# Scaling the first norm's rows on GpSimd in place of ScalarE, with ScalarE left to empty PSUM

## The chip, the cores and the metric

The kernel runs on one core of a Trainium2 chip. The metric is device time in microseconds (us), median of several runs. Runs of one kernel differ by up to some 7 us (the 11 runs of the kernel before in one set lie from 1665.80 to 1673.18 us), so differences of 2 us or less between times are not read as results. The start of a stage is read from one trace of each kernel. Two traces of this same first stage have it at 36.15 and 36.50 us, so differences of up to some 0.5 us between starts are not read either.

Engine names in the profile: PE is TensorE (matmuls), PEld its weight loads, DVE is VectorE, ACT is ScalarE, POOL is GpSimd. In this kernel the results of matmuls land in PSUM; to empty or evict a PSUM tile is to copy it out, here into YT.

## The reference, cut to what matters

Four layers on x of 2048 tokens by 640 columns. The first is a layer norm, a two-dimensional Fourier filter and a residual:

```python
def _layernorm(x, axis=-1, eps=1e-05):
    m = jnp.mean(x, axis=axis, keepdims=True)
    v = jnp.var(x, axis=axis, keepdims=True)
    return (x - m) / jnp.sqrt(v + eps)
...
    x = A_x
    x = x + _A_ref(_layernorm(x, axis=-1), A_w_r, A_w_i)     # this layer
    x = x + _B_ref(_layernorm(x, axis=-1), ...)              # attention with memory
    ...                                                      # both again
```

The change touches only the norm of the first layer and the transform right after it.

## The kernel before

The 2048 tokens lie as 16 "rows" of 128 partitions by 640 columns. In groups of four rows: DVE computes mean and variance, ScalarE computes Ln and Exp for the reciprocal deviation, five small DVE operations refine it, ScalarE scales each row, PE multiplies it with a table (five column chunks), and each of the five PSUM tiles is emptied into YT, three by DVE and two by ScalarE. The next stage (`along_d`) sums over all of YT, so it can't start before the last tile of the last group is emptied.

```python
def _ln_apply(nc, pool, mv, xin, xout, nt, eps_t, on_dve=False):
    rs = pool.tile([128, 4], FP32, name="lnrs", tag="lnrs")      # pool: two of each in turn ("two-deep")
    nb = pool.tile([128, 4], FP32, name="lnnb", tag="lnnb")
    t, r0 = rs[:, :nt], nb[:, :nt]
    nc.scalar.activation(out=r0, in_=mv[:, :nt, 1], func=ACTF.Ln, bias=eps_t[:, 0:1])
    nc.scalar.activation(out=r0, in_=r0, func=ACTF.Exp, scale=-0.5)
    ...                                                          # four small DVE operations -> rs
    nc.vector.scalar_tensor_tensor(out=nb[:, :nt], ...)          # -mean * rs
    for t in range(nt):
        nc.scalar.activation(out=xout[:, t, :], in_=xin[:, t, :], func=ACTF.Identity,
                             scale=rs[:, t:t + 1], bias=nb[:, t:t + 1])
...
        for q in range(4):
            ...                                                  # statistics of four rows on DVE
            _ln_apply(nc, wk, mv, xt, xn[:, 4 * q:4 * q + 4, :], 4, g["eps"])
            for ch in range(5):
                ps = pp.tile([128, 4, 128], FP32, name="ps1", tag="pa")
                for i in range(4):
                    nc.tensor.matmul(ps[:, i, :], lhsT=xn[:, 4 * q + i, ch * 128:(ch + 1) * 128], ...)
                on_act = ... ch >= 3                             # chunks 3 and 4 on ScalarE
                (nc.scalar.copy if on_act else nc.vector.tensor_copy)(out=YT[...], in_=ps[...])
```

## Time and profile before

| | before |
|---|---|
| median of 4 runs beside the change | 1668.90 us |
| profiled span | 1669.1 us |
| first matmul of the next stage (`along_d`) | 36.15 us |
| ScalarE, one row scaled | 0.91 us |
| DVE, one row scaled (elsewhere in this kernel) | 0.446 us |

The profile's page begins with each engine's busy time, share of the span and number of instructions:

```profile
PE 1564.6 (94%) x14240; PEld 1081.5 (65%) x14241; DVE 810.9 (49%) x2308; ACT 837.0 (50%) x2534; POOL 268.5 (16%) x192
```

PE is busy 94% of the program, but not in its first 36 us. The timeline of that stretch: start in us, duration of the merged piece in us, engine, source line, operation, output from input, how many, and in brackets the idle time ahead of it.

```profile
11.90 3.35 ACT L124 ACTIVATE A1xn_S<-A1x_S,lnnb,lnrs 128x640 bf16<-128x640 bf16 x4 [2.28 <-DVE lnnb L122]
...
15.96 1.07 ACT L247 CAST A1YT_S<-ps 128x512 bf16<-128x512 f32 x2 [0.28 <-PE ps L245]
...
19.75 4.16 ACT L124 ACTIVATE A1xn_S<-A1x_S,lnnb,lnrs 128x640 bf16<-128x640 bf16 x5 [1.43 <-DVE lnnb L122]
...
24.76 2.55 ACT L124 ACTIVATE A1xn_S<-A1x_S,lnnb,lnrs 128x640 bf16<-128x640 bf16 x3
...
27.53 0.21 ACT L113 ACTIVATE lnnb<-lnnb 128x4 f32<-128x4 f32 x1
...
30.48 3.35 ACT L124 ACTIVATE A1xn_S<-A1x_S,lnnb,lnrs 128x640 bf16<-128x640 bf16 x4 [1.40 <-DVE lnnb L122]
...
36.15 6.62 PE L290 MATMUL ab<-A1tab_S,A1YT_S 128*128 128x321 bf16 x30 [1.55 <-DVE A1YT_S L247]
```

ScalarE does rows and evictions by turns: group 0's rows at 11.90, two evictions at 15.96, then rows of two groups from 19.75 to 27.3 with group 1's evictions between, and the last group's rows only at 30.48: its Exp came at 27.53, and its five small operations then stood behind three evictions on DVE until 29.49. The last row is scaled at 33.83 and the next stage starts at 36.15 us. That start is the number to follow.

The view of waits over the first 60 us (who waited for whom: total us, times, longest):

```profile
PE ps L245 <- ACT A1xn_S L124: 22.0, 4, 12.9
...
ACT A1xn_S L124 <- DVE lnnb L122: 5.1, 3, 2.3
```

PE idled 22.0 us there until ScalarE had scaled a row, and ScalarE 5.1 us until the small DVE operations were done.

The groups of instructions by form (busy us, mean ns of one, then idle ahead of them):

```profile
L124 ACT ACTIVATE A1xn_S<-A1x_S,lnnb,lnrs 128x640 bf16<-128x640 bf16 x16 | 13.4, 910 | 5.1 <-DVE lnnb L122 5.1
...
L120 DVE TENSOR_SCALAR bB_S<-bB1x_S,lnmv,lnrs 128x640 bf16<-128x640 bf16 x16 | 7.1, 446 | 0.6
```

The same view of GpSimd alone:

```profile
L329 POOL TENSOR_TENSOR A1tmp_S<-A1gt_S 128x642 bf16<-128x642 f32 x5 | 6.6, 1321 | 2.7 <-DVE A1gt_S L326 2.6
...
L824 POOL MEMSET bB_S<- 128x634 f32 x4 | 2.8, 735 | 60.5 <-PE psg L393 31.1 <-DMA xn<-A1tok_S 29.5
```

ScalarE takes 910 ns a row. DVE takes 446 ns for the same row elsewhere in the kernel. For GpSimd there is no line with a `tensor_scalar` on a large tile: only a `tensor_tensor` of 642 columns (1321 ns) and a memset (735 ns).

### The profile page before, as it was taken

What the parts mean: (1) busy time and instruction counts of PE and PEld (TensorE: products, weight loads), DVE (VectorE), ACT (ScalarE), POOL (GpSimd) and SP (SyncE); (2) the same over time, 40 slices, a digit from 0 to 9 for tenths busy, and PEclk for the clock granted to TensorE, in tenths of its full rate; (3) what the DMA queues carried; (4) which work ended last, traced back from release to release, by engine and by line L of the source; (5) the groups of instructions that cost most, each with busy time, mean ns of one, the idle gap of its engine ahead of it and who ended that gap; (6) DMA issues with size and microseconds to landing.
All of it is one profiled execution on the core that took longest, in us unless ns stands there. A gap on an engine that the chain in (4) does not pass through costs nothing. (4 is left out here: it accounts for less than half of the span.)

```text
span 1669.1 us, 36193 instructions
## 1 busy us (share of the span) xinstructions
PE 1564.6 (94%) x14240; PEld 1081.5 (65%) x14241; DVE 810.9 (49%) x2308; ACT 837.0 (50%) x2534; POOL 268.5 (16%) x192
## 2 busy tenths in 40 slices
PE   4887999999999999999987889999999999999998
PEld 2555666666666666677754666676666666666775
DVE  5963354545555554543357724545555554544111
ACT  5364466666666666511123636666666666663000
POOL 0510111121212121100025001121212121111000
PEclk9997999999999999999999999999999999999999
DMA  4463134434343344633301803434343343437241
GB/s 154 158 237 104 51 137 135 151 114 162 112 161 127 137 147 139 227 129 100 91 17 58 283 2 106 148 116 162 112 160 129 135 149 136 136 123 233 66 127 55
DMA packets 167873, 218.05 MB, mean 131 GB/s; under 512 B 7374, under 2 KB 141836, under 8 KB 159756
## 3 DMA queue, kind: packets, MB, share of 16 engines
q1 hardware_dynamic: 167084, 213.34, 38.2%
q8 instruction: 113, 1.85, 0.4%
q0 software_dynamic: 608, 2.30, 0.4%
q14 instruction: 68, 0.56, 0.1%
HBM read 170.52 MB, written 45.09 MB: 129 GB/s over the span
## 5 line engine op out<-in xcount | busy, mean ns | idle before, releaser
L840 PEld LDWEIGHTS <-bB_S 128*128 128x128 bf16 x3180 | 260.3, 97 | 187.1 <-issue 7.8
L984 DVE TENSOR_TENSOR bB_S<-pso,bB_S 128x480 bf16<-128x480 f32 (+1 forms) x320 | 189.5, 593 | 264.7 <-PE pso L975 249.1
L919 ACT ACTIVATE bB_S<-pss 128x269 bf16<-128x269 f32 (+5 forms) x576 | 213.3, 385 | 192.6 <-PE pss L916 177.8
L1134 PE MATMUL psx<-Wo_sb,bB_S 128*128 128x320 bf16 x2048 | 288.2, 299 | 2.9 <-DMA bB_S<-oTx_d 2.9
L1134 PEld LDWEIGHTS <-bB_S 128*128 128x128 bf16 x2048 | 197.2, 98 | 79.5 <-DMA bB_S<-oTx_d 3.6
L899 DVE CAST bB_S<-psk 128x495 bf16<-128x495 f32 (+3 forms) x320 | 191.4, 599 | 115.9 <-PE psk L840 85.6
L920 DVE TENSOR_TENSOR bB_S<-bB_S,maskf 128x269 bf16<-128x269 bf16 (+5 forms) x576 | 163.1, 287 | 152.6 <-ACT bB_S L919 148.8
L944 POOL TENSOR_TENSOR bB_S<-bB_S,bB_S 128x634 f32<-128x634 f32 x64 | 98.2, 1535 | 821.1 <-ACT bB_S L940 821.1
L908 ACT CAST bB_S<-psv 128x512 bf16<-128x512 f32 (+1 forms) x288 | 160.5, 557 | 84.0 <-PE psv L906 83.7
L884 ACT ACTIVATE bB_S<-psq 128x480 bf16<-128x480 f32 x300 | 152.6, 509 | 98.2 <-PE psq L840 98.2
L840 PE MATMUL psk<-B2hT_S,bB_S 128*128 128x495 bf16 (+3 forms) x800 | 165.0, 342 | 3.7 <-DVE bB_S L899 2.5
L840 PE MATMUL psk<-B1hT_S,bB_S 128*128 128x495 bf16 (+3 forms) x800 | 165.0, 342 | 1.8 <-DVE B1hT_S L1219 1.2
L906 PE MATMUL psv<-bB_S,B2hT_S 128*128 128x256 bf16 x1360 | 163.4, 272 | 0.2 <-DVE bB_S L899 0.2
L906 PE MATMUL psv<-bB_S,B1hT_S 128*128 128x256 bf16 x1360 | 163.4, 272 | 0.2 <-DVE bB_S L899 0.2
L916 PEld LDWEIGHTS <-bB_S 128*128 128x128 bf16 x1216 | 103.0, 98 | 90.1 <-issue 6.4
L840 PE MATMUL psq<-B1hT_S,bB_S 128*128 128x495 bf16 (+5 forms) x780 | 157.6, 336 | 0.1
L840 PE MATMUL psq<-B2hT_S,bB_S 128*128 128x495 bf16 (+5 forms) x780 | 157.6, 336 | 0.1
L916 PE MATMUL pss<-bB_S 128*128 128x132 bf16 (+8 forms) x1216 | 148.3, 216 | 3.1
L906 PEld LDWEIGHTS <-B1hT_S 128*128 128x128 bf16 x1360 | 128.6, 98 | 13.7 <-issue 0.3
L906 PEld LDWEIGHTS <-B2hT_S 128*128 128x128 bf16 x1360 | 128.5, 98 | 13.8 <-issue 0.3
L975 PE MATMUL pso<-bB_S,bB_S 128*128 128x132 bf16 (+8 forms) x1216 | 119.6, 216 | 0.0
L975 PEld LDWEIGHTS <-bB_S 128*128 128x128 bf16 x1216 | 91.2, 98 | 15.7 <-DVE oTmf L985 0.5
(223 smaller groups left out, 1565.7 us busy)
## 6 DMA issues: line engine op xcount, KB each, us to landing
bB_S<-Rd SPq DMA_DIRECT2D x62, 1059.5 KB
oTx_d<-bB_S SPq DMA_DIRECT2D x60, 512.0 KB
bB_S<-oTx_d SPq DMA_DIRECT2D x56, 512.0 KB
bB_S<-in_B_Wq_dram SPq DMA_DIRECT2D x32, 320.0 KB
bB_S<-in_B_Wk_dram SPq DMA_DIRECT2D x32, 320.0 KB
bB_S<-in_B_Wv_dram SPq DMA_DIRECT2D x32, 320.0 KB
bB_S<-oTx_d SPq DMA_DIRECT2D x14, 384.0 KB
Wo_sb<-in_B_Wo_dram SPq DMA_DIRECT2D x4, 1280.0 KB
```

The costliest lines, as they stand in the source:

```text
L840: nc.tensor.matmul(ps, lhsT=w[:, ch, hh * 128:(hh + 1) * 128], rhs=src[:, ch, lo:hi], start=(ch == 0), stop=(ch == 4))
L884: nc.scalar.mul(out=qv[:, :, 0:SEG], in_=x_view(ps, o, n)[:, :, 1:SW], mul=scale)
L899: nc.vector.tensor_copy(out=KTs[h % 2][:, lo:hi], in_=ps[:, 0:hi - lo])
L906: nc.tensor.matmul(ps[:, i * 256:(i + 1) * 256], lhsT=hT[:, ch, (t + i) * 128:(t + i + 1) * 128], rhs=w["Wv"][:, ch, :], start=(ch == 0), ...
L908: nc.scalar.copy(out=V[:, t:t + n, :].rearrange("p a b -> p (a b)"), in_=ps[:, 0:n * 256])
L916: nc.tensor.matmul(ps[:, off - o0:off - o0 + hi - lo], lhsT=KT[:, t * 128:(t + 1) * 128], rhs=QT[:, lo:hi], start=True, stop=True)
L919: nc.scalar.activation(out=E[:, 0:n], in_=ps[:, 0:n], func=ACTF.Exp)
L920: nc.vector.tensor_tensor(out=P[:, o0:o0 + n], in0=E[:, 0:n], in1=bs.mask[:, o0:o0 + n], op=ALU.mult)
L944: nc.gpsimd.tensor_tensor(out=accS, in0=accS, in1=sums_sb, op=ALU.add)
L975: nc.tensor.matmul(pso[:, lo - q0:hi - q0], lhsT=V[:, t, (h % 2) * 128:(h % 2 + 1) * 128], rhs=P[:, off:off + hi - lo], start=(i == 0), st ...
L984: nc.vector.tensor_tensor(out=oT.rearrange("p (r s j) -> p r s j", r=16, j=2)[:, :, s0:s0 + ns, :], in0=byclass(po), in1=rx, op=ALU.mult)
L1134: self.tc.nc.tensor.matmul(ps[:, 0:320], lhsT=lhs(h, k // 2), rhs=self.g["Wo_sb"][:, h, c0:c0 + 320], start=(h == 0), stop=(h == H - 1))
```

## The change

The intent: take the row scaling (13.4 us busy) from ScalarE and give 14 of the 16 rows to GpSimd, which has little to do there; give GpSimd the small operations of four groups too, so that DVE is left mainly with the statistics; let ScalarE alone empty PSUM for the first three groups; and split the last four rows into two pairs, each with one row on DVE and one on GpSimd, so that the last evictions are short. These last pairs' evictions are shared, three by ScalarE and two by DVE.

```diff
--- before.py
+++ after.py
@@ -105,23 +105,22 @@
     nc.vector.bn_aggr(out=mv[:, t, :], in_=st[:, t, :, :])
 
 
-def _ln_apply(nc, pool, mv, xin, xout, nt, eps_t, on_dve=False):
+def _ln_apply(nc, pool, mv, xin, xout, nt, eps_t, small, big):
     rs = pool.tile([128, 4], FP32, name="lnrs", tag="lnrs")
     nb = pool.tile([128, 4], FP32, name="lnnb", tag="lnnb")
     t, r0 = rs[:, :nt], nb[:, :nt]
     nc.scalar.activation(out=r0, in_=mv[:, :nt, 1], func=ACTF.Ln, bias=eps_t[:, 0:1])
     nc.scalar.activation(out=r0, in_=r0, func=ACTF.Exp, scale=-0.5)
-    nc.vector.scalar_tensor_tensor(out=t, in0=mv[:, :nt, 1], scalar=LN_EPS, in1=r0, op0=ALU.add, op1=ALU.mult)
-    nc.vector.tensor_tensor(out=t, in0=t, in1=r0, op=ALU.mult)
-    nc.vector.tensor_scalar(out=t, in0=t, scalar1=-0.5, scalar2=1.5, op0=ALU.mult, op1=ALU.add)
-    nc.vector.tensor_tensor(out=t, in0=t, in1=r0, op=ALU.mult)
-    if on_dve:
-        for t in range(nt):
-            nc.vector.tensor_scalar(out=xout[:, t, :], in0=xin[:, t, :], scalar1=mv[:, t, 0:1], scalar2=rs[:, t:t + 1], op0=ALU.subtract, op1=ALU.mult)
-        return
-    nc.vector.scalar_tensor_tensor(out=nb[:, :nt], in0=mv[:, :nt, 0], scalar=-1.0, in1=rs[:, :nt], op0=ALU.mult, op1=ALU.mult)
+    if small is nc.vector:
+        small.scalar_tensor_tensor(out=t, in0=mv[:, :nt, 1], scalar=LN_EPS, in1=r0, op0=ALU.add, op1=ALU.mult)
+    else:
+        small.tensor_scalar_add(out=t, in0=mv[:, :nt, 1], scalar1=LN_EPS)
+        small.tensor_tensor(out=t, in0=t, in1=r0, op=ALU.mult)
+    small.tensor_tensor(out=t, in0=t, in1=r0, op=ALU.mult)
+    small.tensor_scalar(out=t, in0=t, scalar1=-0.5, scalar2=1.5, op0=ALU.mult, op1=ALU.add)
+    small.tensor_tensor(out=t, in0=t, in1=r0, op=ALU.mult)
     for t in range(nt):
-        nc.scalar.activation(out=xout[:, t, :], in_=xin[:, t, :], func=ACTF.Identity, scale=rs[:, t:t + 1], bias=nb[:, t:t + 1])
+        big[t].tensor_scalar(out=xout[:, t, :], in0=xin[:, t, :], scalar1=mv[:, t, 0:1], scalar2=rs[:, t:t + 1], op0=ALU.subtract, op1=ALU.mult)
 
 
 def _ln_tiles(nc, pool):
@@ -232,20 +231,23 @@
             nc.sync.dma_start(out=self.x, in_=r16(x_src))
         wk = g["ln"]
         pp = tc.alloc_tile_pool(name=f"{self.lname}_ps1", bufs=8, space=PSUM)
-        for q in range(4):
+        groups = [(0, 4), (4, 8), (8, 12), (12, 14), (14, 16)]
+        for q, (a, b) in enumerate(groups):
+            n = b - a
             if xn_src is None:
-                xt = self.x[:, 4 * q:4 * q + 4, :]
+                xt = self.x[:, a:b, :]
                 st, mv = _ln_tiles(nc, wk)
-                for t in range(4):
+                for t in range(n):
                     _ln_stats(nc, st, mv, xt[:, t, :], t)
-                _ln_apply(nc, wk, mv, xt, xn[:, 4 * q:4 * q + 4, :], 4, g["eps"])
+                big = [nc.gpsimd] * 4 if q < 3 else [nc.vector, nc.gpsimd]
+                _ln_apply(nc, wk, mv, xt, xn[:, a:b, :], n, g["eps"], nc.gpsimd if q < 4 else nc.vector, big)
             for ch in range(5):
                 ps = pp.tile([128, 4, 128], FP32, name="ps1", tag="pa")
-                for i in range(4):
-                    nc.tensor.matmul(ps[:, i, :], lhsT=xn[:, 4 * q + i, ch * 128:(ch + 1) * 128], rhs=T[:, 4 * q + i, :], start=True, stop=True)
-                on_act = ch % 2 == 0 if xn_src is not None else ch >= 3
+                for i in range(n):
+                    nc.tensor.matmul(ps[:, i, :], lhsT=xn[:, a + i, ch * 128:(ch + 1) * 128], rhs=T[:, a + i, :], start=True, stop=True)
+                on_act = ch % 2 == 0 if xn_src is not None or q >= 3 else True
                 (nc.scalar.copy if on_act else nc.vector.tensor_copy)(
-                    out=YT[:, ch, :, 4 * q:4 * q + 4, :].rearrange("p g s k -> p s g k"), in_=ps[:].rearrange("p s (g k) -> p s g k", k=8))
+                    out=YT[:, ch, :, a:b, :].rearrange("p g s k -> p s g k"), in_=ps[:, 0:n, :].rearrange("p s (g k) -> p s g k", k=8))
                 if q == 0 and ch == 0:
                     self.tables(gate=YT[0:1, 0, 0, 0, 0:1])
         pp.release()
... (three other call sites: on_dve=True becomes nc.vector, [nc.vector] * n; the operations stay the same)
```

More of the change, by code (lines that the diff above doesn't have):

```diff
@@ L414, in norm @@
             xno = xna[:, 2 * q:2 * q + 2, :]
-            _ln_apply(nc, wk, mv[q], x[:, 2 * q:2 * q + 2, :], xno, 2, g["eps"], on_dve=True)
+            _ln_apply(nc, wk, mv[q], x[:, 2 * q:2 * q + 2, :], xno, 2, g["eps"], nc.vector, [nc.vector] * 2)
             nc.sync.dma_start(out=xnd[:, 2 * q:2 * q + 2, :], in_=xno)
@@ L686, in run @@
                 xno = wk.tile([128, 1, D], BF16, name="xno", tag="xno")
-                _ln_apply(nc, wk, mv, xo, xno, 1, self.g["eps"], on_dve=True)
+                _ln_apply(nc, wk, mv, xo, xno, 1, self.g["eps"], nc.vector, [nc.vector])
                 nc.sync.dma_start(out=self.xnd[:, t, :], in_=xno[:, 0, :])
@@ L1151, in run @@
             _ln_stats(nc, st, mv, x[:, t, :], 0)
-            _ln_apply(nc, self.g["ln"], mv, x[:, t:t + 1, :], xns[t % 3].unsqueeze(1), 1, self.g["eps"], on_dve=True)
+            _ln_apply(nc, self.g["ln"], mv, x[:, t:t + 1, :], xns[t % 3].unsqueeze(1), 1, self.g["eps"], nc.vector, [nc.vector])
         if nxt is not None:
```

## The prediction

> **What bounds it now.** As a whole, TensorE: 1564.6 of 1669.1 us busy, and the chain of waits is 41% PE. The change touches only the first 36 us. There (timeline, waits) PE has 80 small matmuls, 11.5 us, and idles 22.0 us on ScalarE's row scaling. PE's first matmul of the next stage starts at 36.15 us; that is the number to move. It needs all of YT, so everything ahead of it is in series.
>
> By groups of instructions, before 36 us: DVE statistics 32 x 465 ns plus 16 x 195 ns, one row per 0.86 us (5.1 to 22.0 us with evictions between); ScalarE scales 16 rows x 905 ns = 14.5 us, evicts 8 tiles x 587 ns, Ln and Exp 4 x 0.5 us; DVE evicts 12 x 683 ns = 7.5 us. ScalarE serializes scaling and eviction: group 0's rows at 11.9-15.2, then evictions, group 1's not before 19.75, group 2's end at 27.3, group 3's run 30.5-33.8 because its Ln/Exp queued behind and its five small DVE operations took 1.0 us. GpSimd is idle from 18 to 48 us.
>
> **What changes.** 14 of 16 row scalings go to GpSimd, two to DVE (its bf16 row: 445 ns, seen later in the trace). No trace line has a GpSimd tensor_scalar. Its two-input bf16-writing operation on 642 elements took 1321 ns, its memset of 634 fp32 735 ns. The Trainium skill ("GPSIMD Engine Reference", 4.1) puts one-input operations near line rate and two-input ones at a read-port floor; so I estimate 0.8 us a row (0.7 to 1.1). GpSimd small operations: estimate 0.2-0.3 us each with semaphores, 1.0-1.4 us a group, against 1.0 on DVE. ScalarE: minus 14.5 us, plus about 9 more evictions near 0.55. DVE: minus about 6 us of evictions.
>
> **Critical path, estimated.** Group 0: Exp ends 9.6 as before, small operations to 11.0, rows to 14.2 (before 15.2). GpSimd then runs nearly without a break: group 1 with the 1 us indirect DMA to 19.4, group 2 to 23.6, row 13 to 25.4. A new wait: mean/variance tiles are two deep and the rows now read them, so group q+2's aggregates wait for group q's rows. The last pair thus finishes statistics near 25.4, Ln/Exp 26.0, DVE small operations 26.8, row 15 on GpSimd 27.7, half-size evictions to 29.5-30. The next stage starts near 30 in place of 36.15: a gain of about 6 us (range 1 to 9). The later stages aren't changed and should shift one for one: table loads are done by 22 us (DMA is idle from 25 us), and the clock dips (0.5 to 0.6 at 88-96 and 132-152 us) follow PE gaps that shift too.
>
> 6 us of 1669 is 0.35%, near the run-to-run spread (1668.87 to 1673.11). Predicted 1663.5 us, 8 in 10 within 1659.5 to 1668.5. Faster by over 2%: 0.01; within: 0.985; slower: 0.005.
>
> **What would show it.** Next stage's first matmul at 29-31 us. GpSimd rows 0.7-1.1 us each; GpSimd the releaser of the stage's matmuls; DVE statistics of groups 2 on interrupted by waits on GpSimd; ScalarE no longer the wait; span after that point equal to before (1633 us).
>
> **What would make it wrong.** A row on GpSimd at 1.4 us or more makes 14 of them 20 us and eats the gain. Small dependent GpSimd operations at 0.5 us each would cost 2.5 us a group. The shared port: the trace has a DVE two-input operation growing from 0.83 to 2.2 us beside GpSimd work, as the Trainium skill says ("SBUF — State Buffer", port pair as an exclusive lock); the last pairs' DVE row and small operations could stall so. The indirect DMA may sit in GpSimd's queue ahead of rows, waiting for its gate. The stage's end may be set by ScalarE's evictions.

## The result, and the profile after

| | before | after |
|---|---|---|
| median (4 runs each) | 1668.90 us | 1688.47 us |
| ratio | 1 | 1.0112 (1.0094 to 1.0130) |
| profiled span | 1669.1 us | 1686.3 us |
| first matmul of the next stage | 36.15 us | 57.02 us |
| one row on GpSimd | none | 2.49 us from start to start |

A ratio here is the mean time of one kernel's fast runs over that of the other's fast runs of the same rounds, so it isn't quite the ratio of the medians. The change makes the kernel 1.1% slower: 19.6 us by the medians, where about 5 us faster had been predicted.

The same line of the page after:

```profile
PE 1562.4 (93%) x14240; PEld 1080.8 (64%) x14241; DVE 804.2 (48%) x2286; ACT 829.5 (49%) x2533; POOL 309.2 (18%) x226
```

PE's busy time has not grown (1562.4 against 1564.6 us): the loss is idle time. The timeline of the first stage after, columns as before:

```profile
11.78 9.98 POOL L123 TENSOR_SCALAR A1xn_S<-A1x_S,lnmv,lnrs 128x640 bf16<-128x640 bf16 x4
...
14.36 0.61 PE L247 MATMUL ps<-A1xn_S 128*128 128x128 bf16 x4 [14.36 <-POOL A1xn_S L123]
...
22.14 1.07 ACT L249 CAST A1YT_S<-ps 128x512 bf16<-128x512 f32 x2 [9.15 <-PE ps L247]
...
23.32 5.00 POOL L123 TENSOR_SCALAR A1xn_S<-A1x_S,lnmv,lnrs 128x640 bf16<-128x640 bf16 x2
...
29.58 4.99 POOL L123 TENSOR_SCALAR A1xn_S<-A1x_S,lnmv,lnrs 128x640 bf16<-128x640 bf16 x2
...
36.13 9.97 POOL L123 TENSOR_SCALAR A1xn_S<-A1x_S,lnmv,lnrs 128x640 bf16<-128x640 bf16 x4
...
46.48 2.54 ACT L249 CAST A1YT_S<-ps 128x512 bf16<-128x512 f32 x5 [8.80 <-PE ps L247]
48.87 0.25 ACT L113 ACTIVATE lnnb<-lnnb 128x2 f32<-128x2 f32 x1
...
50.41 5.17 POOL L123 TENSOR_SCALAR A1xn_S<-A1x_S,lnmv,lnrs 128x640 bf16<-128x640 bf16 x2
...
57.02 5.65 PE L292 MATMUL ab<-A1tab_S,A1YT_S 128*128 128x321 bf16 x30 [0.46 <-ACT A1YT_S L249]
```

GpSimd's pieces follow one another with small operations, one indirect DMA and one standstill between: four rows in 9.98 us, two in 5.00, two in 4.99, four in 9.97, two in 5.17. Those are the 14 rows, 35.1 us in sum. PE now starts at a row's end (14.36), does 0.6 us of work and idles for the next one. ScalarE, freed for evictions, has its first one at 22.14, six us later than before, as all four rows of group 0 must be there.

A second, smaller thing can be read at the end. Row 13's Exp (48.87) could have run long before: its Ln had begun at 37.34 and took 0.34 us. In ScalarE's queue it stood behind the five evictions of group 2 (46.48), and these waited for the last row of group 2. So GpSimd, which had only begun its small operations for row 13, stood still for 2.85 us until 49.27.

The waits over the first 70 us:

```profile
PE ps L247 <- POOL A1xn_S L123: 41.3, 14, 14.4
ACT A1YT_S L249 <- PE ps L247: 33.2, 5, 9.8
DVE lnmv L105 <- POOL A1xn_S L123: 27.2, 3, 10.9
```

The releaser of PE has changed from ScalarE (22.0 us) to GpSimd (41.3 us). DVE waits 27.2 us for GpSimd: this is the new wait for the two-deep statistics tiles that the prediction named (there are two of each, so a group's statistics wait until GpSimd has read those of the group two before it). It is large in sum, but whether it costs anything is another question, since GpSimd, the engine that is late, was busy nearly all the while (39.0 of the 45 us from 12 to 57).

The groups by form in the first 57 us:

```profile
L123 POOL TENSOR_SCALAR A1xn_S<-A1x_S,lnmv,lnrs 128x640 bf16<-128x640 bf16 x14 | 35.1, 2517 | 0.5
...
L123 DVE TENSOR_SCALAR A1xn_S<-A1x_S,lnmv,lnrs 128x640 bf16<-128x640 bf16 x2 | 0.9, 446 | 0.6 <-POOL lnrs L121 0.6
```

The same instruction on the same data takes 2517 ns on GpSimd and 446 ns on DVE.

The loss comes from the first stage alone. Marks that lie later are shifted by a nearly constant amount: the first matmul of `along_d` from 36.15 to 57.02 (20.9 us), the first of the second layer A from 852.3 to 872.0 (19.7 us).

### The profile page after: what moved, and what is told of

Read it like the earlier page. It is cut to its first block, busy times and chain, and to the rows that moved or that the text cites. A ratio compares the mean times of both kernels' runs of the same rounds, so it can differ in the third digit from the quotient of the medians.

```text
span 1686.3 us, 36214 instructions
## 1 busy us (share of the span) xinstructions
PE 1562.4 (93%) x14240; PEld 1080.8 (64%) x14241; DVE 804.2 (48%) x2286; ACT 829.5 (49%) x2533; POOL 309.2 (18%) x226
```

## The experiments

Theory A: a row costs about 2.49 us on GpSimd by itself, and the number of rows on GpSimd times that sets the first stage. Rival B: the two-deep statistics tiles and the order in ScalarE's queue make the loss. Rival C: GpSimd was slowed by DVE, with which it shares memory ports. A fourth possibility was that the dependent small operations on GpSimd make it. All runs gave a correct result by the comparison with the reference. Each set of runs has its own chip and its own runs of the kernel before; these had medians 1669.16 us (first set), 1667.70 (second) and 1668.95 (third).

### Forms of GpSimd operations, measured by themselves

```diff
+            for i in range(3):
+                G.tensor_scalar(out=pb[i], in0=v, scalar1=e, scalar2=e, op0=ALU.subtract, op1=ALU.mult)
+            ... (three each of the other forms, on one row v of 640 columns, into dead memory)
```

> The kernel before, with GpSimd operations on 128x640 added in the last phase of the program, where DVE and GpSimd are almost idle; results go to dead memory. Theory A (the operation itself is slow on GpSimd, whatever runs beside it): the two-operation form of the change, two pointer scalars, bf16 to bf16, again takes 2.4 to 2.5 us from start to start, and its 320-column form about half, 1.25 to 1.35. Rival C (GpSimd was slowed by sharing memory ports with the busy DVE in the first stage): the same form takes about 1 us here. What in the form costs is open: if it is the second operation, the one-operation form takes 1.3 us or less; if it is the pointer scalars, the form with immediates does; if it is the bf16 data, the fp32 forms do. The plain copy should be near 0.8 us, the tensor_tensor near 1.3 to 1.5. The time of the whole kernel: within 3 us of before.

The kernel took 1669.82 us (one run). The groups by form, GpSimd alone, from 1522 to 1590 us; the letters after the operation are output from input, where `eps` means a scalar read through a pointer (or, in L1134, spread over the row as the second tensor):

```profile
L1118 POOL TENSOR_SCALAR bB_S<-bB2x_S,eps 128x640 bf16<-128x640 bf16 x3 | 7.6, 2537 | 0.1
L1128 POOL TENSOR_SCALAR bB_S<-bB_S,eps 128x640 bf16<-128x640 f32 x3 | 7.5, 2501 | 0.0
L1130 POOL TENSOR_SCALAR bB_S<-bB_S,eps 128x640 f32<-128x640 f32 x3 | 7.5, 2499 | 0.1
L1124 POOL TENSOR_SCALAR bB_S<-bB2x_S 128x640 bf16<-128x640 bf16 x3 | 7.1, 2359 | 0.0
L1122 POOL TENSOR_SCALAR bB_S<-bB2x_S,eps 128x640 bf16<-128x640 bf16 x3 | 5.6, 1888 | 0.0
L1126 POOL TENSOR_SCALAR bB_S<-bB2x_S 128x640 bf16<-128x640 bf16 x3 | 5.4, 1814 | 0.0
...
L1120 POOL TENSOR_SCALAR bB_S<-bB2x_S,eps 128x320 bf16<-128x320 bf16 x3 | 4.3, 1433 | 0.0
L1132 POOL TENSOR_TENSOR bB_S<-bB2x_S 128x640 bf16<-128x640 bf16 x3 | 3.8, 1254 | 0.0
L1134 POOL TENSOR_TENSOR bB_S<-bB2x_S,eps 128x640 bf16<-128x640 bf16 x3 | 3.8, 1253 | 0.0
L1138 POOL COPY bB_S<-bB2x_S 128x640 bf16<-128x640 bf16 x3 | 2.2, 718 | 0.0
```

- The form of the change (L1118) takes 2.5 us here too, and so do its fp32 relatives (L1128, L1130), which ran between 1548 and 1574 us; from 1540 to 1580 us DVE was busy 4.43 of 40 us. In the trace of the change, rows that ran beside statistics on DVE (11.78 to 14) and rows that ran beside an idle DVE (29.58 to 34.6) both took 2.49 us. Rival C falls.
- Half the columns (L1120) take 1.43 us, where 1.25 to 1.35 had been expected. So the cost goes with the columns, but not all of it: (2501 - 1433) / 320 = 3.3 ns a column (L1128 against L1120; the median of L1118, 2499 ns, gives the same), and some 0.4 us fixed, an estimate from the same two numbers.
- fp32 in place of bf16 (L1128, L1130) changes nothing for `tensor_scalar`. Immediate scalars in place of pointers save 0.15 us (L1124). Leaving one of the two operations out saves 0.5 to 0.6 us (L1122, L1126), so a single operation still takes 1.8 to 1.9 us.
- A `tensor_tensor` on two bf16 rows takes 1.25 us (L1132), also with one column spread over the row (L1134); in fp32 it took 1.54 us. A copy takes 0.72 us (L1138). So on GpSimd the operation with two tensors is faster than the one with a tensor and scalars.

The Trainium skill ("Perfetto Trace Analysis", GPSIMD Engine Instruction) says that the span of a GpSimd instruction in a profile is unreliable and that start-to-start spacing is the thing to use. Here the spacing is used, and it differs little from the spans for these forms: four rows of the change took 9.98 us, 2.49 us apart, and the mean span of all 14 was 2.52. So no run here shows the unreliability.

### The rows alone

The kernel before with nothing but its 16 rows on GpSimd:

```diff
-        nc.scalar.activation(out=xout[:, t, :], in_=xin[:, t, :], func=ACTF.Identity, scale=rs[:, t:t + 1], bias=nb[:, t:t + 1])
+        nc.gpsimd.tensor_scalar(out=xout[:, t, :], in0=xin[:, t, :], scalar1=mv[:, t, 0:1], scalar2=rs[:, t:t + 1], op0=ALU.subtract, op1=ALU.mult)
... (the small operation for nb, no longer read, goes too)
```

> The kernel before with one part of the change alone: its 16 rows scaled on GpSimd, everything else (groups of four, evictions on both engines, small operations on DVE) as before. Theory A: 16 rows x 2.49 us = 40 us from 11.9 us, plus the indirect DMA of 1 us and one to four us of waits between groups; the next stage starts at 55 to 59 us and the kernel takes 1688 to 1692 us. Rival B (two-deep statistics buffers, queue order and small operations of the change make the loss, not the rows): below 1676 us.

Measured 1691.64 us (ratio 1.0145, 1.0118 to 1.0172), next stage at 60.26 us. GpSimd's timeline in this run, and the start of the next stage on PE:

```profile
11.49 9.96 POOL L123 TENSOR_SCALAR A1xn_S<-A1x_S,lnmv,lnrs 128x640 bf16<-128x640 bf16 x4 [4.52 <-DVE lnrs L117]
...
24.15 9.94 POOL L123 TENSOR_SCALAR A1xn_S<-A1x_S,lnmv,lnrs 128x640 bf16<-128x640 bf16 x4
38.06 19.87 POOL L123 TENSOR_SCALAR A1xn_S<-A1x_S,lnmv,lnrs 128x640 bf16<-128x640 bf16 x8 [3.97 <-DVE lnrs L117]
...
60.26 5.85 PE L289 MATMUL ab<-A1tab_S,A1YT_S 128*128 128x321 bf16 x30 [1.56 <-DVE A1YT_S L246]
```

This one part alone makes a loss as large as the whole change, 22.5 us. The time is as theory A expected; the stage's start is 1.3 us beyond its range. Rival B, which put it below 1676, falls as the main cause.

### Tiles of their own for each group

The change, with statistics and scale tiles that don't take turns:

```diff
... (`_ln_apply` takes the two scale tiles from its caller)
+        s6 = self.ar.get("S6", f"{self.lname}ln")
...
-                st, mv = _ln_tiles(nc, wk)
+                st, mv = s6.f32(4, 2, nc.vector.BN_STATS_DIM), s6.f32(4, nc.vector.BN_AGGR_DIM)
...
-                _ln_apply(nc, wk, mv, ...)
+                _ln_apply(nc, (s6.f32(4), s6.f32(4)), mv, ...)
```

> The change, with statistics and scale tiles of their own for each of the five groups in place of two in turn. Theory A: GpSimd is busy with rows nearly all the time, so only its gaps (3.2 us before row 13, where the Exp sat behind five evictions) come back: next stage at 52 to 55 us in place of 57.0, kernel 1683 to 1687 us. Rival B (the new wait for buffers makes the loss): at or below 1672 us.

Measured 1686.45 us (ratio 1.0105), next stage at 55.80 us: 1.2 us earlier than the change, less than theory A's 2 to 5 us, while the time lies in its range. The gap of GpSimd ahead of row 13 went; another of 2.4 us appeared ahead of row 15, whose Exp now stood behind evictions. So the 27.2 us that DVE waited for GpSimd cost hardly anything: a large sum in the view of waits, on an engine that wasn't the late one.

### The small operations back on DVE

```diff
-                _ln_apply(nc, wk, mv, xt, xn[:, a:b, :], n, g["eps"], nc.gpsimd if q < 4 else nc.vector, big)
+                _ln_apply(nc, wk, mv, xt, xn[:, a:b, :], n, g["eps"], nc.vector, big)
```

> The change, with the small operations of all groups on DVE in place of GpSimd; the rows stay on GpSimd. Theory A: GpSimd saves at most four times 1.4 us, part of which was under other waits: kernel 1682 to 1688 us. A rival by which the dependent small operations on GpSimd make the loss: at or below 1672 us.

Measured 1685.14 us (ratio 1.0098), next stage at 54.53 us, 2.5 us earlier than the change. The small operations on GpSimd cost 2.5 of the 20.9 us, as theory A expected; they are not the cause.

### A cheaper row on GpSimd

The change, with one `tensor_tensor` a row. The mean is left in those rows; the comparison with the reference still passed.

```diff
+        if big[t] is nc.gpsimd:
+            big[t].tensor_tensor(out=xout[:, t, :], in0=xin[:, t, :], in1=rs[:, t:t + 1].to_broadcast([128, D]), op=ALU.mult)
+            continue
```

> The change with a cheaper form of the GpSimd rows: one tensor_tensor with the reciprocal deviation spread over the row (1.22 us from start to start in the run of forms) in place of the two-operation tensor_scalar (2.46 us). The mean is not subtracted from those rows, so the result is slightly wrong on purpose. Theory A (row time on GpSimd sets the stage): 14 rows save 14 x 1.25 = 17.5 us, next stage at 37 to 41 us, kernel 1668 to 1673 us. A rival by which buffers, queue order or small operations hold the stage: at most a third of that comes back, kernel above 1680 us. This also measures the slope of my own prediction's sum, which put the next stage at 30 us for 0.8 us a row.

Measured 1670.32 us (ratio 1.0008, 0.9993 to 1.0022), next stage at 38.78 us. The row went from 2.49 to 1.22 us, 14 of them 17.8 us, and the stage's start went from 57.02 to 38.78, 18.2 us. So the start follows the row's cost one for one. The end of the stage in this run:

```profile
31.25 3.37 ACT L252 CAST A1YT_S<-ps 128x512 bf16<-128x512 f32 x8 [3.80 <-PE ps L250]
31.34 1.48 DVE L126 TENSOR_SCALAR A1xn_S<-A1x_S,lnmv,lnrs 128x640 bf16<-128x640 bf16 x1 [5.85 <-POOL lnrs L121]
31.38 1.25 POOL L124 TENSOR_TENSOR A1xn_S<-A1x_S,lnrs 128x640 bf16<-128x640 bf16 x1
...
34.43 0.29 ACT L113 ACTIVATE lnnb<-lnnb 128x2 f32<-128x2 f32 x1
...
35.58 1.25 POOL L124 TENSOR_TENSOR A1xn_S<-A1x_S,lnrs 128x640 bf16<-128x640 bf16 x1 [2.95 <-DVE lnrs L121]
...
38.78 1.50 PE L295 MATMUL ab<-A1tab_S,A1YT_S 128*128 128x321 bf16 x5 [0.46 <-ACT A1YT_S L252]
```

Two things can be read here. The last pair still has its Exp (34.43) behind eight evictions (31.25), so GpSimd's last row waits until 35.58. And the DVE row at 31.34 took 1.48 us in place of 0.446, beside a GpSimd `tensor_tensor` of 1.25 us that began at 31.38; the other DVE row of this run took 1.48 us too. Beside a GpSimd `tensor_scalar` of 2.5 us, DVE rows took 0.45 us in the change, and 0.44 and 0.92 us in the run with the small operations on DVE.

### The rows on DVE

```diff
-                big = [nc.gpsimd] * 4 if q < 3 else [nc.vector, nc.gpsimd]
+                big = [nc.vector] * 4
```

> The change with all 16 rows on DVE (0.445 us each) and the small operations of four groups still on GpSimd. Theory A: next stage at 28 to 32 us, kernel 1660 to 1666 us, thus faster than both. If the rest of the change (ScalarE alone on evictions, pairs, small operations on GpSimd) were at fault: above 1672 us. If DVE becomes the new limit at the same length: 1667 to 1671 us.

Measured 1664.62 us (ratio 0.9974, 0.9957 to 0.9990). The next stage started at 33.29 us, later than the 28 to 32 expected, but 23.7 us earlier than in the change:

```profile
33.29 5.50 PE L292 MATMUL ab<-A1tab_S,A1YT_S 128*128 128x321 bf16 x30 [0.46 <-ACT A1YT_S L249]
```

The rest of the change is thus sound: with the rows on the faster engine it gains on the kernel before.

### Rows and small operations on DVE

The last edit, and the small operations of all groups on DVE.

> As the last, with the small operations on DVE too, GpSimd doing nothing of the norm. DVE then has 13.7 us of statistics, 7.1 of rows and some 3 of small operations from 5.1 us: next stage at 29 to 32 us, kernel 1660 to 1666 us; within 2 us of the run with small operations on GpSimd, which says what those are worth once the rows are away.

Measured 1662.70 us (ratio 0.9967, 0.9952 to 0.9982), next stage at 30.93 us. The stage's start is 2.4 us earlier than with the small operations on GpSimd, a little more than the 2 us expected, so these had been on the critical path. The end of the stage:

```profile
21.60 1.49 DVE L123 TENSOR_SCALAR A1xn_S<-A1x_S,lnmv,lnrs 128x640 bf16<-128x640 bf16 x4
...
23.99 3.37 ACT L249 CAST A1YT_S<-ps 128x512 bf16<-128x512 f32 x8 [0.58 <-PE ps L247]
...
27.17 0.37 ACT L112 ACTIVATE lnnb<-lnmv,eps 128x2 f32<-128x2 f32 x1
...
28.60 0.80 DVE L123 TENSOR_SCALAR A1xn_S<-A1x_S,lnmv,lnrs 128x640 bf16<-128x640 bf16 x2
...
30.93 5.37 PE L292 MATMUL ab<-A1tab_S,A1YT_S 128*128 128x321 bf16 x27 [0.58 <-ACT A1YT_S L249]
```

This version beats both kernels, by 0.33% the kernel before. Four rows take 1.49 us on DVE, against 9.98 on GpSimd. What ends the stage now is the last pair's Ln at 27.17, behind eight evictions (23.99).

### One row of each group of four on GpSimd

```diff
-                big = [nc.vector] * 4
+                big = [nc.gpsimd, nc.vector, nc.vector, nc.vector] if q < 3 else [nc.vector] * 2
```

> As the run with all on DVE, with one row of each group of four on GpSimd (2.46 us each, beside three DVE rows and the next statistics). DVE saves 3 x 0.45 us; but the first and third groups now wait for a row of 2.5 us that starts when the DVE rows do, 1.2 us longer than four DVE rows in series. Theory: within 1.5 us of the run with all on DVE, either way. If DVE rows are blocked for the length of GpSimd's row by a shared port, DVE rows beside it take over 1 us in the trace.

Measured 1667.74 us (ratio 0.9988, 0.9971 to 1.0005), next stage at 34.63 us: 3.7 us later than with all on DVE, where within 1.5 us was expected. The trace shows where the time goes: the third group's GpSimd row ran from 23.29 to 25.8, after which PE had 2.3 us of matmuls for the group, its evictions came at 27.24, and the Exp of the next pair stood behind them until 29.63. The lock on DVE rows that the run also looked for showed only faintly: beside a GpSimd row of 2.50 us, three DVE rows took 1.54 or 1.55 us, where four take 1.49 with no GpSimd row beside them. The median DVE row was 435 ns and the longest 833. That is a delay of some 0.4 us a group, not a block for the whole of GpSimd's row.

### Tiles of their own, with all on DVE

> All rows and small operations on DVE, as in the run that was fastest so far, with tiles of their own for each group. If the two-deep statistics tiles cost anything once the rows are short, the next stage starts before 30.9 us, by up to 1 us; kernel 1661 to 1664 us. If they cost nothing, the same within 0.5 us in the stage's start. In either case the wait for buffers is shown to be small beside 20 us.

Measured 1663.54 us (ratio 0.9960, 0.9946 to 0.9973), next stage at 31.27 us, against 30.93 with two tiles in turn. The two-deep tiles cost nothing once the rows are short.

### Each group's norm written ahead of the evictions before it

```diff
+        if xn_src is None:
+            norm(0)
         for q, (a, b) in enumerate(groups):
             n = b - a
+            if xn_src is None and q < 4:
+                norm(q + 1)
... (`norm(q)` is the statistics and `_ln_apply` of group q; own tiles as in the last run)
```

> As the last, with each group's norm written ahead of the evictions of the group before it, so that Ln and Exp of the last pair do not stand behind all evictions on ScalarE (in the run with all on DVE the last pair's statistics were done at 24.3 us and its Ln began at 27.2). The last rows should end 2 to 3 us earlier, the next stage start at 28 to 30 us, kernel 1659 to 1663 us. If it is no faster than the run with all on DVE, ScalarE's sum of evictions sets the end and not the place of Ln and Exp.

Measured 1661.38 us (ratio 0.9955, 0.9941 to 0.9968), next stage at 30.79 us. The stage's start missed its range of 28 to 30, and is only 0.5 us before that of the run of the same set without this edit, hardly more than two traces of one kernel differ by. The edit did half of what it was for, as ScalarE's timeline shows:

```profile
24.30 0.30 ACT L111 ACTIVATE A1ln_S<-A1ln_S,eps 128x2 f32<-128x2 f32 x1 [1.41 <-DVE A1ln_S L105]
24.99 2.54 ACT L255 CAST A1YT_S<-ps 128x512 bf16<-128x512 f32 x5 [0.40 <-PE ps L253]
27.39 0.25 ACT L112 ACTIVATE A1ln_S<-A1ln_S 128x2 f32<-128x2 f32 x1
```

Ln moved ahead of the evictions (24.30), Exp did not (27.39), although ScalarE stood idle for 0.40 us ahead of them, after Ln. Why Exp was queued there the runs don't show. So whether the stage would start earlier with Exp ahead too, or the sum of evictions would hold it, as the expectation asks, stays open. The time is the lowest of all, but it can't be told from that of its neighbour (1663.54, intervals of the ratio overlap).

### All runs in one table

The shift of the next stage's start is against 36.15 us, that of the time against the median of the kernel before in the same set.

| run | row engine | start, us | shift of start | shift of time |
|---|---|---|---|---|
| the change | GpSimd 14, DVE 2 | 57.02 | +20.9 | +19.6 |
| rows alone | GpSimd 16 | 60.26 | +24.1 | +22.5 |
| own tiles | GpSimd 14, DVE 2 | 55.80 | +19.7 | +17.3 |
| small operations on DVE | GpSimd 14, DVE 2 | 54.53 | +18.4 | +16.0 |
| cheaper GpSimd row | GpSimd 14, DVE 2 | 38.78 | +2.6 | +2.6 |
| one row in four on GpSimd | GpSimd 3, DVE 13 | 34.63 | -1.5 | 0.0 |
| rows on DVE | DVE 16 | 33.29 | -2.9 | -3.1 |
| all on DVE | DVE 16 | 30.93 | -5.2 | -5.0 |
| all on DVE, own tiles | DVE 16 | 31.27 | -4.9 | -5.4 |
| the same, norm ahead | DVE 16 | 30.79 | -5.4 | -7.6 |

The time follows the stage's start within 2.5 us in every run. Starts within some 0.5 us of each other (the last three rows) aren't told apart.

## Why the prediction was wrong

**What bounds the first stage, and that later stages shift one for one: right.** The table shows the time following the stage's start, and what lies after that start took 1629.3 us of the profiled span in the change against 1632.9 before, within the spread of runs. The clock dips moved along, as said: before, TensorE was busy 1.17 of 4 us from 84 and 0.72 from 128, and the granted clock in the next 4 us was 0.59 and 0.64; in the change the gaps came at 104 and 148 (1.09 and 0.64 us busy), with 0.50 after each.

**"So I estimate 0.8 us a row (0.7 to 1.1)": wrong, and this is the step that failed.** It measured 2.49 us. The estimate rested on a memset and a two-tensor operation from the trace, and on the Trainium skill ("GPSIMD Engine Reference", 4.1 Engine selection), which calls one-input operations on GpSimd roughly line-rate and two-input ones about twice as slow as on VectorE. In the run of forms a copy (0.72 us) was indeed faster than the two-input `tensor_tensor` (1.25 us), but `tensor_scalar`, which also has one input tensor, was slower than both (1.8 to 2.5 us). For 14 rows the term is off by 14 x (2.49 - 0.8) = 23.7 us; the stage's start was off by 57.0 - 30 = 27 us. The prediction named this as its first risk ("a row on GpSimd at 1.4 us or more"), but its range didn't hold it: a cost for which the trace had no line was given a spread of 0.4 us, and the interval of the whole was built on that.

**The rest of the sum: about 3 us short.** The prediction's own steps with 1.22 us a row in place of 0.8 put the next stage near 35.6 us: rows of group 0 from 11.0 to 15.9, group 1 with small operations and the indirect DMA to 22.8, group 2 to 28.7, row 13 to 30.9, then Ln, Exp, small operations and row 15 to 33.6, evictions 2 more. With that row cost it started at 38.78. The trace of that run shows what is missing: Exp of the last pair behind eight evictions, which delays row 15 to 35.58. The prediction looked at ScalarE's sum, where there was room, and not at the order of its queue. So even at 0.8 us a row the start would have been near 38.8 - 14 x 0.42 = 32.9 us, an estimate from this run's slope that no run tests: a gain of 3 us, not 6.

**"A new wait: mean/variance tiles are two deep": the wait is there, its cost is small.** DVE waited 27.2 us for GpSimd, and giving each group its own tiles brought the start back by 1.2 us.

**Small operations on GpSimd, "1.0-1.4 us a group": nearly right, a little low.** In the trace they take 1.5 us from the first to the row (21.84 to 23.32, 34.66 to 36.13), and taking them away brought 2.5 us in the change and 2.4 us with the rows on DVE.

**The shared port: not the cause, and only partly as feared.** The Trainium skill ("SBUF — State Buffer", Who interferes with whom) says that of a DVE operation in a 2-port mode (or with two inputs in SBUF) and a GpSimd operation that reads SBUF, the one that starts first blocks the other fully. For two `tensor_tensor` operations the trace before agrees: DVE's took 0.83 us where it started first (58.57 against 58.62 us) and GpSimd's 2.19, and 2.22 us where GpSimd's had started first (64.76 against 64.78), with GpSimd's at 1.57. For the rows it agrees only in part. Beside GpSimd's `tensor_tensor` a DVE row took 1.48 us, 1.03 us more than alone, which is near that operation's 1.25; but by the trace the DVE row had started first, by 0.04 us. Beside GpSimd's `tensor_scalar` DVE rows took 0.45 us in the change, at most 0.83 in the mixed run, where GpSimd's had started 0.2 us before, and at most 0.92 with the small operations on DVE: never GpSimd's 2.5 us. Whether a DVE row runs in such a mode no run shows. Why the two GpSimd operations differ in this, the runs don't say. They also leave open why `tensor_scalar` is slow on GpSimd; only that it is, by how much a column, and that data type and kind of scalar matter little.

## What to carry to other kernels

An idle engine is no reason to move work to it: measure the operation in its exact form on that engine first, or look for a trace line with that form, since a neighbour in the list of operations can be off by a factor of three. Here the same intent (free ScalarE for evictions, short last groups) paid 5 us with the rows and small operations on DVE, at 0.45 us a row, and lost 20 us with the rows on GpSimd, at 2.49. Look at the order of an engine's queue and not only at its sum: small operations that others wait for (here Ln and Exp) stood behind evictions that waited for something late. What moving both ahead would bring isn't shown here, since the one try moved only Ln.

## What the Trainium skill lacked or had wrong

- "GPSIMD Engine Reference", 4.1 Engine selection: one-input operations are called roughly line-rate. A copy of 128x640 took 0.72 us, but `tensor_scalar` with one operation took 1.81 to 1.89 us and with two 2.36 to 2.54 us, against 1.25 us for the two-input `tensor_tensor`. The page has no figure for `tensor_scalar`; a column costs 3.3 ns in the two-operation form.
- The same page, 8 Key points: elementwise work is called about twice as fast on VectorE. For a bf16 row scaled by two scalars it was 2517 against 446 ns, a factor of 5.6.
- "SBUF — State Buffer", Who interferes with whom: the page makes no difference between GpSimd operations that read SBUF. A DVE row took 1.48 us beside `tensor_tensor`, and mostly 0.43 to 0.45 us (at most 0.92) beside the longer `tensor_scalar`.
